# The attention softmax of a fused kernel: normalising multiplies of two blocks on GpSimd, and their weight copy shared by ScalarE and VectorE

## The chip, the cores and the metric

One core of a Trainium2 chip runs the whole program. The metric is device time in microseconds. An engine is named as in the profile: PE is TensorE (PEld its weight loads), DVE is VectorE, ACT is ScalarE, POOL is GpSimd, SP is SyncE, which issues the DMAs here.

## The reference

Windowed causal attention, then two feed-forward layers, all in float32.

```python
scores = q @ k.T / sqrt(64) - slope[h] * (i - j)        # 4 batches, 8 heads, 576 positions
scores = where(0 <= i - j < 128, scores, -1e9)
attn = exp(scores - max); attn = attn / (sum(attn) + 1e-9)
x = concat_heads(attn @ v)                              # 2304 tokens x 512
h = x @ w_in;  x = (h * clip(h + 3, 0, 6) / 6) @ w_out  # 512 -> 2048 -> 512
xn = x / rms(x) * rms_g
out = (silu(xn @ w_gate) * (xn @ w_val)) @ w_out2       # 512 -> 1536 -> 512
```

## The kernel before

The 2304 tokens are 18 tiles of 128 rows, in six blocks of three tiles. Attention works on a pair of heads (`Pair`, four to a block) and one tile of queries (`Step`, three to a pair); both heads of the pair lie side by side in every tile. A step looks at 256 columns of keys (its own tile and the one before), some at 128 or 192 because a batch begins there. One step goes through these pieces, each a method:

- `scores`: q times k on PE, into PSUM.
- `bias` (L367): a DVE instruction for each head adds the slope and the mask and finds the row's extreme `m`.
- `exp` (L382): an ACT instruction for each head gives exp and its row sum `den`. Then POOL makes the reciprocal `r`: an add (L384) and a power of -1 (L385), both on 128x2 values.
- `divide` (L390): each head's tile `t` is multiplied by its column of `r`.
- `transpose` (L396): PE turns `t` into the one PSUM tile `ps_t`.
- `weights` (L401): `ps_t` is copied to SBUF as `pt`.
- `values` (L414): PE multiplies by v.

Every engine takes its instructions in the order in which the code emits them; nothing reorders them. Time is cut into slots by hand. In the first two blocks (pairs 0 to 7, 24 steps) one step begins in each slot, and a step's pieces lie one slot apart: scores, bias and exp in slot t, divide in t+1, transpose and weights in t+2, values in t+3. Slots 0 to 14 are a prologue with attention alone, besides some conversions of weights. From slot 15 on a slot also holds one chunk m of the first feed-forward layer of block 0: `product1` (L480, into `ps_h`), the activation (L717 on ACT, L718 on DVE), its split into a high and a low part (L723 on ACT, L729 on DVE) and `product2` (L493). So the divides of the first two blocks fall into slots 1 to 24, ten of them in the feed-forward loop.

In each of these slots a further tile of weights is converted as well, by ACT (L129, L134, L143) and DVE (L138, L141, L145); `product2` needs the low part that L145 writes. The weights arrive by DMA (L161) from SP, whose queue also loads q, k and v: a load waits there until its buffer is free, and what stands behind it waits too.

Blocks 2 to 5 have a slower plan and masks of another kind (`joint`); they keep their code.

Of the kernel before, what the change touches and what calls it, by code (L numbers as in the profile page):

```python
# [16 lines left out]
ALU = mybir.AluOpType  # L17
# [3 lines left out]
P = 128  # L21
# [50 lines left out]
def fused_kernel(ctx: ExitStack, tc: tile.TileContext, qd, kd, v, w1, w2, rms_g, out):  # L72
# [7 lines left out]
    vec, act, pool, pe, sp = nc.vector, nc.scalar, nc.gpsimd, nc.tensor, nc.sync  # L80
# [245 lines left out]
    class Step:  # L326
# [60 lines left out]
        def divide(self):  # L387
            for a in range(2):
                p = self.t[:, a, self.p0 :]
                vec.tensor_scalar(p, p, self.r[:, a : a + 1], None, ALU.mult)  # L390

        def transpose(self):
            self.ps = ps_a.tile([P, 2, 2, P], F32, tag="T", name="ps_t")
# [4 lines left out]
        def weights(self):  # L398

            self.pt = ap.tile([P, 2, 2, P], F32, tag="pt", name="pt", bufs=3)  # L400
            act.copy(self.pt[:, :, self.p0 // P :], self.ps[:, :, self.p0 // P :])  # L401
            for c, sign in ((0, -1), (1, 1)) if self.joint else ():
                pool.affine_select(  # L403
                    out=self.pt[:, :, c], in_=self.pt[:, :, 1], compare_op=ALU.is_ge, fill=0.0,
                    base=c - 1, pattern=[[0, 2], [sign, P]], channel_multiplier=-sign,
                )
# [592 lines left out]
```

## Time and profile before

| | us |
|---|---|
| median of three runs | 962.07 |
| lowest and highest of them | 959.27, 962.39 |
| the profiled execution | 959.62 |
| its span in the trace | 957.9 |

The profiled execution takes 1.72 us more than its span. A timeline row gives start, duration, engine, line, operation, tiles written and read, count, and in brackets how long the engine had been idle before and what ended that. The chain of waits is followed back from the last instruction: each piece is what the next one waited for.

### The profile page before, as it was taken

The page shows a single profiled execution, that of the slowest core. Times are in us where ns is not written, and L with a number is a line of the kernel's source. Part 1 is how long each engine was busy: PE and PEld are TensorE (multiplying, and loading weights), DVE is VectorE, ACT ScalarE, POOL GpSimd, SP SyncE. Part 2 cuts the span into 40 slices and gives each one's busy share as a digit, 9 for nine tenths or more (in the row PEclk, how much of TensorE's full clock was granted, in tenths as well). Part 3 has the DMA queues.
Part 4 walks back from the last instruction along what each step waited for, and adds up shares of the span by engine and source line. Part 5 has one row for each costly group of instructions (what it writes and reads, how often), then busy time and mean ns, then how long its engine had stood idle before and what let it go on. Part 6 is the DMA issues. An engine that isn't in the chain of part 4 may idle for free.

```text
span 957.9 us, 14648 instructions
## 1 busy us (share of the span) xinstructions
PE 938.1 (98%) x5336; PEld 831.6 (87%) x5336; DVE 642.0 (67%) x1336; ACT 453.6 (47%) x969; POOL 185.2 (19%) x327
## 2 busy tenths in 40 slices
PE   7799899999999999999999999999999999999998
PEld 4587788888888888888898989999999999999996
DVE  5788765555778777877477657777545577545555
ACT  6899764454656655665455453433232323231120
POOL 4333012332223322332034323310000000000000
PEclk8999999999999999999999999999999999999999
DMA  6445601113666554554346757866657655755521
GB/s 225 173 163 192 231 20 33 48 43 108 197 205 218 171 174 144 169 166 154 121 157 232 264 210 281 326 243 233 237 214 283 214 212 200 264 202 209 214 89 67
DMA packets 67432, 175.02 MB, mean 183 GB/s; under 512 B 5024, under 2 KB 41888, under 8 KB 62624
## 3 DMA queue, kind: packets, MB, share of 16 engines
q1 hardware_dynamic: 67360, 174.09, 52.2%
q8 instruction: 42, 0.69, 0.3%
q14 instruction: 30, 0.25, 0.1%
HBM read 130.03 MB, written 44.04 MB: 182 GB/s over the span
## 4 chain that ended last, share of the span: by engine, by line
PE 87%; DVE 5%; ACT 4%; issue 2%; POOL 1%; DMA 1%; SPq 0%; ACTq 0%; POOLq 0%; DVEq 0%
PE ps_o L493 19%; PE ps_h L480 18%; PE ps_y L886 15%; PE ps_o L839 10%; PE ps_S L839 8%; PE ps_A L839 6%; PE ps_h L839 4%; PE ps_av L414 3%; PE ps_t L396 2%; PE ps_s L344 1%; PE ps_s L353 1%; ACT t L382 1%; ACT wx L134 1%; PE ps_x L545 1%; DVE wx L141 1%
## 5 line engine op out<-in xcount | busy, mean ns | idle before, releaser
L493 PE MATMUL ps_o<-w,g 128*128 128x512 f32 x864 | 224.7, 402 | 3.8 <-DVE w L145 2.6
L480 PE MATMUL ps_h<-xs,w 128*128 128x384 f32 x1152 | 220.3, 339 | 0.0
L480 PEld LDWEIGHTS ps_h<-xs,w 128*128 128x128 f32 x1152 | 202.2, 188 | 6.3 <-DVE t L718 0.6
L493 PEld LDWEIGHTS ps_o<-w,g 128*128 128x128 f32 x864 | 156.1, 188 | 43.6 <-DVE w L145 6.0
L886 PE MATMUL ps_y<-wo,g 128*128 128x512 f32 x648 | 150.2, 390 | 0.5 <-DVE g L875 0.5
L886 PEld LDWEIGHTS ps_y<-wo,g 128*128 128x128 f32 x648 | 121.4, 188 | 25.1 <-DVE g L875 0.9
L718 DVE SCALAR_TENSOR_TENSOR t<-t,ps_h 128x384 f32<-128x384 f32 x96 | 53.1, 553 | 99.0 <-ACT t L717 99.0
L717 ACT ACTIVATE t<-ps_h,three 128x384 f32<-128x384 f32 x96 | 55.3, 576 | 79.3 <-PE ps_h L480 76.1
L893 DVE TENSOR_TENSOR y<-y,ps_y 128x512 f32<-128x512 f32 x90 | 61.6, 685 | 35.3 <-PE ps_y L886 35.0
L382 ACT ACTIVATE t<-t,m 128x128 f32<-128x128 f32 (+1 forms) x144 | 61.2, 426 | 29.7 <-DVE t L374 13.5
L723 ACT CAST g<-t 128x384 fp32r<-128x384 f32 x96 | 49.4, 514 | 48.7 <-DVE t L718 47.1
L729 DVE TENSOR_TENSOR g<-t,g 128x384 fp32r<-128x384 f32 x96 | 55.1, 574 | 23.0 <-ACT g L723 22.6
L862 ACT ACTIVATE r<-r 128x384 f32<-128x384 f32 x36 | 18.9, 526 | 105.9 <-DVE r L861 105.9
L839 PE MATMUL ps_o<-S,tw 128*128 128x384 f32 x336 | 66.1, 338 | 0.3 <-DVE t L859 0.3
L384 POOL TENSOR_SCALAR r<-den 128x2 f32<-128x2 f32 x72 | 27.5, 382 | 190.0 <-ACT t L382 188.5
L839 PEld LDWEIGHTS ps_o<-S,tw 128*128 128x128 f32 x336 | 59.3, 188 | 1.2 <-DVE t L859 0.6
L385 POOL TENSOR_TENSOR r<-r,minus 128x2 f32<-128x2 f32 x72 | 55.8, 775 | 6.0
L403 POOL TENSOR_SCALAR_AFFINE_SELECT pt<-pt 128x256 f32<-128x256 f32 x82 | 35.4, 432 | 108.6 <-ACT pt L401 105.6
L847 ACT COPY s<-ps_S 128x384 f32<-128x384 f32 x18 | 8.6, 480 | 88.0 <-PE ps_S L839 88.0
L367 DVE CUSTOM_DVE_ANT_0 t<-ps_s,rel 128x256 f32<-128x256 f32 (+2 forms) x128 | 45.2, 395 | 4.1 <-PE ps_s L353 4.1
L141 DVE SCALAR_TENSOR_TENSOR wx<-wx,wy 128x512 uint32<-128x512 uint32 (+1 forms) x52 | 44.2, 849 | 0.0
L134 ACT ACTIVATE wx<-wraw 128x512 f32<-128x512 f32 (+1 forms) x52 | 42.8, 823 | 0.0
(138 smaller groups left out, 1468.5 us busy)
## 6 DMA issues: line engine op xcount, KB each, us to landing
tw<-t SPq DMA_DIRECT2D x52, 896.0 KB, 6.3
wraw<-w SPq DMA_DIRECT2D x36, 512.0 KB, 4.2
wo<-w SPq DMA_DIRECT2D x18, 1024.0 KB, 4.9
wraw<-w SPq DMA_DIRECT2D x16, 1024.0 KB, 8.4
t<-th SPq DMA_DIRECT2D x12, 896.0 KB, 4.5
t<-tl SPq DMA_DIRECT2D x12, 896.0 KB, 4.2
b<-wx SPq DMA_DIRECT2D x24, 256.0 KB, 2.5
w<-w SPq DMA_DIRECT2D x12, 512.0 KB, 3.0
```

The lines of the kernel that those rows point to most:

```text
L134: act.activation(x, high.bitcast(F32), AF.Copy, scale=2.0**-112)
L141: vec.scalar_tensor_tensor(out=xi, in0=xi, scalar=3, in1=y, op0=ALU.logical_shift_left, op1=ALU.bitwise_or)
L382: act.activation(p, p, AF.Exp, bias=self.m[:, a : a + 1], scale=-1.0, accum_out=self.den[:, a : a + 1])
L385: pool.tensor_tensor(self.r, self.r, minus, ALU.pow)
L480: pe.matmul(ps[:, : n * P], lhsT=w[:, a, c * P : (c + 1) * P], rhs=xs[c][:, b, : n * P], start=(k == 0), stop=(k == 3 * KC - 1),)
L493: pe.matmul(o, lhsT=g[:, a, i * P : (i + 1) * P], rhs=w[:, b], start=(m == first and a == 0 and b == 0), stop=(m == last and a == 1),)
L717: act.activation(r[:, :nq], ps[:, :nq], AF.Relu, bias=three)
L718: vec.scalar_tensor_tensor(out=r[:, :nq], in0=r[:, :nq], scalar=6.0, in1=ps[:, :nq], op0=ALU.min, op1=ALU.mult)
L729: vec.tensor_sub(g[:, 1, :nq], r[:, :nq], f32(g[:, 0, :nq]))
L839: pe.matmul(ps, lhsT=w[a][:, k, c * P : (c + 1) * P], rhs=x[:, b, c], start=(start and j == 0), stop=(j == 5), skip_group_check=True,)
L886: pe.matmul(ps, lhsT=gs[i + k][:, a, t // 3, t % 3 * P : (t % 3 + 1) * P], rhs=wo[i + k][:, b], start=(k == 0 and a == 0 and b == 0), stop ...
L893: vec.tensor_add(acc[t], acc[t], ps)
```

## The change

For blocks 0 and 1 (`pair.b < 2`) the two multiplies of `divide` are issued to POOL and no longer to DVE, and the copy in `weights` is cut by head: ACT copies head 0 and DVE copies head 1. Nothing else moves, and the other blocks are as before. Lines after L401 are numbered up to five higher.

```diff
         def divide(self):
             for a in range(2):
                 p = self.t[:, a, self.p0 :]
-                vec.tensor_scalar(p, p, self.r[:, a : a + 1], None, ALU.mult)
+                (pool if self.pair.b < 2 else vec).tensor_scalar(p, p, self.r[:, a : a + 1], None, ALU.mult)
...
         def weights(self):
...
-            act.copy(self.pt[:, :, self.p0 // P :], self.ps[:, :, self.p0 // P :])
+            c0 = self.p0 // P
+            if self.pair.b < 2:
+                act.copy(self.pt[:, 0, c0:], self.ps[:, 0, c0:])
+                vec.tensor_copy(self.pt[:, 1, c0:], self.ps[:, 1, c0:])
+            else:
+                act.copy(self.pt[:, :, c0:], self.ps[:, :, c0:])
```

On DVE, slots 7 and 8 of the prologue, before (ISA is the bias instruction and its read of `m`):

```order
L367 ISA t,m<-ps_s_369,rel 128x256
L367 ISA m 128x1
L367 ISA t,m<-ps_s_370,rel 128x256
L367 ISA m 128x1
L300 TENSOR_SCALAR qraw<-qraw,qscale 128x384
L390 TENSOR_SCALAR t<-t,r 128x128 x2
L141 SCALAR_TENSOR_TENSOR wx<-wx,wy 128x1024
L367 ISA t,m<-ps_s_398,rel 128x256
```

The same place on DVE now:

```order
L404 COPY pt<-ps_t 128x256
L367 ISA t,m<-ps_s_374,rel 128x256
L367 ISA m 128x1
L367 ISA t,m<-ps_s_375,rel 128x256
L367 ISA m 128x1
L300 TENSOR_SCALAR qraw<-qraw,qscale 128x384
L141 SCALAR_TENSOR_TENSOR wx<-wx,wy 128x1024
L404 COPY pt<-ps_t 128x128
L367 ISA t,m<-ps_s_404,rel 128x256
```

The divide behind the slot's bias is gone, and a copy stands ahead of the slot's bias.

On DVE in a slot of the feed-forward loop (the slot with the rows of 67 us below), before:

```order
L145 TENSOR_TENSOR w<-wx,w 128x1024
L718 SCALAR_TENSOR_TENSOR t<-t,ps_h 128x384
L390 TENSOR_SCALAR t<-t,r 128x256 x2
L367 ISA t,m<-ps_s_901,rel_split 128x256
L367 ISA m 128x1
```

The same place on DVE now (L718 has become L723):

```order
L145 TENSOR_TENSOR w<-wx,w 128x1024
L723 SCALAR_TENSOR_TENSOR t<-t,ps_h 128x384
L404 COPY pt<-ps_t 128x256
L367 ISA t,m<-ps_s_918,rel_split 128x256
L367 ISA m 128x1
```

Between the activation and the bias one copy stands where two multiplies stood.

On POOL at the start of the prologue, before:

```order
L384 TENSOR_SCALAR r<-den 128x2
L385 TENSOR_TENSOR r<-r,minus 128x2
L384 TENSOR_SCALAR r<-den 128x2
L385 TENSOR_TENSOR r<-r,minus 128x2
L384 TENSOR_SCALAR r<-den 128x2
```

On POOL now:

```order
L384 TENSOR_SCALAR r<-den 128x2
L385 TENSOR_TENSOR r<-r,minus 128x2
L390 TENSOR_SCALAR t<-t,r 128x128 x2
L384 TENSOR_SCALAR r<-den 128x2
L385 TENSOR_TENSOR r<-r,minus 128x2
L390 TENSOR_SCALAR t<-t,r 128x256 x2
```

A step's multiplies now follow its own reciprocal directly, ahead of the next step's.

## Rows read from the trace of the kernel before

**Rows 1.** The page: span, and part 1, busy time of each engine.
```profile
span 957.9 us, 14648 instructions
PE 938.1 (98%) x5336; PEld 831.6 (87%) x5336; DVE 642.0 (67%) x1336; ACT 453.6 (47%) x969; POOL 185.2 (19%) x327
```

**Rows 2.** Windows: stretch, length, busy us by engine, clock, DMA share, GB/s.
```profile
20.00:40.00 20.00, 14.05 (x117) 9.03 (x118) 15.54 (x59) 16.73 (x50) 8.63 (x17) 1.00 0.31 92
60.00:80.00 20.00, 19.62 (x118) 15.40 (x115) 17.38 (x37) 18.34 (x34) 6.65 (x7) 1.00 0.60 218
```

**Rows 3.** Chain of waits, one slot of the loop: start, us, what.
```profile
66.52 0.47 ACT t L717
67.02 0.56 DVE t L718
67.57 0.53 DVE t L390 x2
...
72.92 0.47 ACT t L717
```

**Rows 4.** Timeline of PE in one slot of the loop.
```profile
62.65 2.26 PE L480 MATMUL ps_h<-xs,w 128*128 128x384 f32 x12
...
66.49 2.38 PE L493 MATMUL ps_o<-w,g 128*128 128x512 f32 x9
...
68.72 2.28 PE L480 MATMUL ps_h<-xs,w 128*128 128x384 f32 x12
```

**Rows 5.** Timeline, all engines: one turn at the prologue's end.
```profile
35.15 0.52 ACT L382 ACTIVATE t<-t,m 128x256 f32<-128x256 f32 x1
...
36.65 0.70 POOL L385 TENSOR_TENSOR r<-r,minus 128x2 f32<-128x2 f32 x1
...
37.38 0.61 DVE L390 TENSOR_SCALAR t<-t,r 128x256 f32<-128x256 f32 x2 [0.61 <-POOL r L385]
...
37.88 0.63 PE L396 MATMUL ps_t<-ident,t 128*128 128x128 f32 x4 [0.53 <-DVE t L390]
...
38.60 0.58 ACT L401 COPY pt<-ps_t 128x512 f32<-128x512 f32 x1 [0.70 <-PE ps_t L396]
...
39.52 0.46 ACT L382 ACTIVATE t<-t,m 128x192 f32<-128x192 f32 x1
```

**Rows 6.** Line L390 in the whole run: its waits, and who waited for it.
```profile
  POOL r L385: 5.5, 10
...
  PE ps_t L396: 7.0, 7
```

**Rows 7.** Groups by shape, POOL and DVE: count, busy us, mean ns.
```profile
L113 POOL COPY rel_split<-rel 128x256 f32<-128x256 f32 x1 | 0.4, 396 | 0.0
L242 POOL TENSOR_TENSOR tx<-tx 128x256 f32<-128x256 f32 x12 | 9.4, 787 | 0.9
...
L367 DVE CUSTOM_DVE_ANT_0 t<-ps_s,rel 128x256 f32<-128x256 f32 x30 | 11.4, 421 | 2.3 <-PE ps_s L353 2.3
...
L390 DVE TENSOR_SCALAR t<-t,r 128x256 f32<-128x256 f32 x32 | 9.8, 350 | 4.0 <-POOL r L385 4.0
```

**Rows 8.** Timeline of PE, slot 11 of the prologue.
```profile
31.20 0.43 PE L396 MATMUL ps_t<-ident,t 128*128 128x128 f32 x2 [2.37 <-DVE t L390]
```

**Rows 9.** Timeline of POOL and DVE in two slots of the loop.
```profile
64.39 0.96 POOL L385 TENSOR_TENSOR r<-r,minus 128x2 f32<-128x2 f32 x1
...
65.49 1.22 DVE L145 TENSOR_TENSOR w<-wx,w 128x1024 fp32r<-128x1024 f32 x1 [0.17 <-ACT w L143]
...
67.02 0.56 DVE L718 SCALAR_TENSOR_TENSOR t<-t,ps_h 128x384 f32<-128x384 f32 x1 [0.31 <-ACT t L717]
...
75.90 1.22 DVE L141 SCALAR_TENSOR_TENSOR wx<-wx,wy 128x1024 uint32<-128x1024 uint32 x1
...
75.94 1.89 POOL L384 TENSOR_SCALAR r<-den 128x2 f32<-128x2 f32 x1 [3.80 <-ACT t L382]
```

**Rows 10.** Timeline of ACT: the conversion of a tile of weights.
```profile
100.65 1.15 ACT L129 ACTIVATE wy<-wraw 128x1024 uint32<-128x1024 uint32 x1 [1.09 <-DMA wraw<-w]
```

## The prediction

> **What bounds the kernel now.** I read the page first, then the windows, then the chain of waits, then timelines of the two stretches that the change touches. Over the span PE is busy 98% and DVE 67%, ACT 47%, POOL 19% [rows 1]; so for most of the run no other engine matters. The change touches the first 100 us alone, and there the windows say something else: in the prologue (20 to 40 us) PE is busy 14 of 20 us and ACT and DVE 16.7 and 15.5; in the feed-forward loop with attention and conversions (60 to 80 us) PE shows 19.6, ACT 18.3, DVE 17.4, POOL 6.7 [rows 2]. Three engines are nearly full there, and POOL is the idle one. The clock is granted in full in both stretches, so it plays no part.
>
> The chain of waits says which of the three it is. In the loop it runs ACT L717, DVE L718, the two multiplies of L390 (0.53 us), the bias, and so on to the next L717, 6.40 us later [rows 3]. So the multiplies are on the path. But PE is close behind: from product1 to product1 it took 6.07 us in a slot in which it waited for nothing [rows 4]. A loop that gets below 6.07 us becomes PE's. In the prologue the chain goes through one step's pieces in turn: exp on ACT at 35.15, the reciprocal on POOL (done at 36.65 + 0.70 = 37.35), multiplies on DVE from 37.38, transposes from 37.88, the copy on ACT at 38.60, and the exp of the step two slots later at 39.52 [rows 5]. That is a latency chain, and what counts on it is how long each piece takes and what stands ahead of it in its queue, not how full an engine is.
>
> What is saved or lost before about 115 us goes to the end unchanged, since behind it PE runs the same work without a gap. So I add up the two stretches.
>
> **Part 1: the multiplies leave DVE, in the loop.** Ten of the 24 steps have their divide in the loop, so ten slots lose 0.53 us of chain [rows 3] and get the copy of one head in the same place. No row shows a copy out of PSUM on DVE. Nearest is the bias instruction, which reads 128x256 from PSUM in 0.42 us [rows 7]; a pair of multiplies lasts 0.61 us [rows 5] and stands in the chain with 0.53, so neighbours overlap by 0.08 and the copy costs 0.34. It is at least 0.27 (half of 0.53, the price of one multiply), at most 0.42. I take 0.34, since bias reads the same memory. A slot gains 0.53 - 0.34 = 0.19 (0.11 to 0.26), ten slots 1.9.
>
> Not all of it arrives. The slot of 6.07 us was one of three kinds that take turns (a slot without a load's scaling or a block's finish); there PE has no slack, so about three of the ten slots give nothing: 0.6 off. At 100.65 us ACT waited 1.09 us for a tile of weights [rows 10], whose load is released by PE in the slot before last; the time between release and need contains about 1.3 slots, whose 1.3 x 0.19 = 0.25 only lengthens the wait. What is left is 1.9 - 0.6 - 0.25 = 1.05 us gained (0.2 to 2.0).
>
> The multiplies themselves are hidden on POOL here: a reciprocal is ready a whole slot before the transposes that need its product. POOL is busy a third of the time [rows 2], and even 1.6 us for the pair fits. Without that cover each would cost its full time in each slot.
>
> **Part 2: ACT copies half.** In the loop ACT's split of g behind the copy waits for DVE's L718 anyhow, so a shorter copy ends nothing sooner; I cost it at nothing. If L718 were done earlier, it would be worth up to half of the copy's 0.58 us [rows 5] in a slot.
>
> **Part 3: the multiplies on POOL, in the prologue.** No row shows POOL multiplying by a column. One input and one output of 128x256 took POOL 0.40 (the copy), two inputs 0.79 [rows 7]. I take 0.45, the copy and a little for the column and for dispatch, since the multiply too has one large input; ends 0.40 and 0.79. A pair then takes 0.90 where DVE takes 0.61 [rows 5]: 0.29 later. Behind it comes a second loss. The copy on DVE now stands ahead of that slot's bias, and exp comes behind bias; before, exp only stood behind ACT's own copy. Copy 0.34, first bias 0.42 and a hand-over make some 0.85 from transposes to exp, where ACT's copy took 0.55: 0.3 more. So where this chain binds, a turn of two slots loses 0.29 to 0.6.
>
> Where does it bind? PE waited for L390 seven times, 7.0 us in all [rows 6], and only there does a later product come through at once; in other slots conversions on ACT keep the turn longer than the chain. Seven times 0.29 is 2.0, seven times 0.6 is 4.2. Against it stands one place where POOL is better: at 31.20 PE had waited 2.37 us [rows 8] for a divide whose reciprocal was long there, because in DVE's queue a conversion (L145) and a bias stood ahead of it. POOL has neither in its queue. I give back 1.1 of the 2.37, about half, since POOL may have to stand aside while L145 runs; ends 0 and 2.0. DVE's ten waits for the reciprocal, 5.5 us [rows 6], go too, but they return as waits of the copy for the transposes. Prologue: 2.0 - 1.1 = 0.9 us lost (0 to 3).
>
> **The sum.** 0.9 lost and 1.05 gained: -0.15 us. On the profiled execution that is 959.62 - 0.15 = 959.5; on the median, which lies 2.45 us above it, 961.9. The executions shown spread from 959.3 to 962.4, and a new median falls anywhere among them; I say 961.5. About 0.3% (2.9 us) is what a measurement of this kernel can tell from no change, and the sum is far inside it.
>
> **The rivals.**
>
> *A, slower: POOL's multiply is dear.* If the column makes it cost as much as POOL's two-input instruction, 0.79 [rows 7], each of the seven turns loses another 2 x 0.34 = 0.68, together 4.8: 964.3 against the profiled execution, 966.7 against the median. It ends beyond 0.3% from about 0.67 us for a multiply of 128x256 (7 x 2 x 0.22 = 3.1). For it: no row excludes it, and POOL's short power takes 0.70 on two values [rows 5]. Against it: the copy's 0.40. By the Trainium skill (GPSIMD Engine Reference, Key points) elementwise work is about twice as fast on VectorE; as an estimate from that page and the 0.35 of DVE's row the multiply would be 0.70, and the sum 963.0 against the profiled execution.
>
> *B: POOL's multiplies stand in DVE's way.* At 75.94 an add on 128x2 values took POOL 1.89 us, from just after the start of DVE's L141 to the end of the conversion behind it, longer than its neighbour, the power, ever needs when left alone [rows 9]. The two engines thus exclude one another in some instructions. In one kind of slot the power ends at 65.35 and L145 starts at 65.49 [rows 9], so a multiply may slip in first. One puts L145 back by 0.36, two by 0.8; L718 behind had 0.31 to spare [rows 9], so 0.05 or 0.5 is lost, in some four slots up to 2.0. The sum becomes +1.85: 961.5 against the profiled execution, 963.9 against the median. The Trainium skill (SBUF — State Buffer, SBUF: two separate sides) says that VectorE and GpSimd share a pair of ports as an exclusive lock, which whichever begins first holds for the whole instruction; by that rule this loss is real wherever a multiply comes first, and the row of 1.89 us agrees with it.
>
> *C, faster: the engines' fill decides.* If the prologue's turns are set by conversions rather than by latency, POOL's slower multiplies are hidden and only the 1.1 given back counts; if PE's 6.07 us has slack that its modelled ends hide, all 1.9 of the loop arrives. Together -3.0: 956.6 and 959.1. For it: ACT and DVE at 83% and 78% in the prologue [rows 2]. Against it: PE's seven waits.
>
> **How the numbers follow.** The forecast 0.57, of its own range -1.5 to +1.8 us; A 0.15, B 0.12, C 0.16. The range goes from just below C, measured from the median, to between B and A: 958.2 to 965.5; the lowest fifth of C and the dearer half of A are outside. Slower by over 0.3%: nearly all of A and a little of B, 0.16. Faster by over 0.3%: the larger part of C, 0.11. Within: 0.73.
>
> **What would show it.** Part 1: in the loop L718 is followed by a copy of 0.27 to 0.42 us, and three slots take 0.3 to 0.5 us less than before, PE waiting less for L145. Part 3: POOL's multiply of 128x256 at 0.40 to 0.50 us; the first product1 at 39.4 to 40.4 us; bias in the prologue released by the copy, the copy by PE. The wait for weights near 100 us grows by some 0.25 us. A shows as multiplies above 0.65 us and a first product1 beyond 42; B as L145 starting over 0.3 us after ACT's L143; C as a first product1 before 39 us and slots of 6.1 us throughout. The prediction is wrong if the conversions or the loads of weights move onto another path than the one I followed, for instance by a load released so late that ACT waits in every third slot.

## The result and the profile after

The changed kernel takes 970.3 us (median of six, 969.8 to 973.6) against 961.5 for the kernel before in the same rounds: a ratio of 1.0106, 95% interval 1.009 to 1.0123. It is slower by 9 us, and outside the range of 958.2 to 965.5. The profiled execution is the slowest of the six, 973.62 with a span of 971.8; it is 2.6 to 3.8 us longer than the other five, of which there is no trace.

The page: span and part 1, then from part 2 the lines of POOL and of TensorE's granted clock in 40 slices of 24.3 us (compare [rows 1]).

```profile
span 971.8 us, 14658 instructions
...
PE 953.8 (98%) x5336; PEld 839.3 (86%) x5336; DVE 636.8 (66%) x1312; ACT 450.2 (46%) x969; POOL 235.6 (24%) x375
...
POOL 7877411322322322242133133310000000000000
PEclk6589999999999999999999999999999999999999
```

POOL has 50 us more work, more than twice the 22 us that 48 multiplies at the assumed 0.45 would make at most, and in the first slices it is the fullest engine but PE. TensorE's clock is low there. Windows of the changed kernel, columns as in [rows 2], and behind them the first stretch in the kernel before:

```profile
18.00:24.00 6.00, 5.28 (x28) 2.64 (x26) 2.80 (x11) 5.08 (x13) 4.72 (x8) 0.50 0.33 98
...
42.00:48.00 6.00, 5.57 (x26) 2.90 (x26) 2.46 (x11) 2.85 (x10) 5.37 (x9) 0.50 0.06 18
```

```profile
18.00:24.00 6.00, 4.58 (x41) 2.68 (x39) 4.92 (x17) 5.32 (x17) 2.95 (x6) 1.00 0.34 93
```

In these stretches of the prologue POOL is busy 4.7 and 5.4 of 6 us, and the granted clock is 0.50 (of the two levels 1.2 and 2.4 GHz the lower), where before it was 1.00. The timeline of all engines early in the prologue shows what a slot is made of:

```profile
11.04 1.83 POOL L390 TENSOR_SCALAR t<-t,r 128x256 f32<-128x256 f32 x2
...
12.93 0.69 PE L396 MATMUL ps_t<-ident,t 128*128 128x128 f32 x2 [0.21 <-POOL t L390]
12.96 0.22 POOL L384 TENSOR_SCALAR r<-den 128x2 f32<-128x2 f32 x1
13.27 0.72 POOL L385 TENSOR_TENSOR r<-r,minus 128x2 f32<-128x2 f32 x1
...
13.66 0.37 ACT L403 COPY pt<-ps_t 128x256 f32<-128x256 f32 x1 [1.20 <-PE ps_t L396]
14.07 0.42 DVE L404 COPY pt<-ps_t 128x256 f32<-128x256 f32 x1 [2.39 <-ACT pt L403]
14.08 1.83 POOL L390 TENSOR_SCALAR t<-t,r 128x256 f32<-128x256 f32 x2
...
14.41 0.28 DVE L367 CUSTOM_DVE_ANT_0 t<-ps_s,rel 128x128 f32<-128x128 f32 x1
...
14.73 0.40 ACT L382 ACTIVATE t<-t,m 128x128 f32<-128x128 f32 x1 [0.70 <-DVE m L367]
```

Two things are to be seen. The pair of multiplies takes POOL 1.83 us, where DVE took 0.61 [rows 5], and with the add and the power POOL needs 14.08 - 11.04 = 3.04 us for a step: add, power, multiplies, and at once the next add. And the copy on DVE starts not when the transposes are done but when ACT's copy is done (14.07 behind 13.66 + 0.37): its release is ACT's, not PE's. Bias and exp queue behind it.

The waits of DVE over the first 130 us, in total, times, longest, and then those of PE:

```profile
DVE pt L404 <- ACT pt L403: 21.2, 11, 3.1
```

```profile
PE ps_t L396 <- POOL t L390: 6.8, 10, 2.0
```

Eleven times DVE's half of the copy was released by ACT's half. The 21.2 us are all of DVE's idle time ahead of these copies, and most of it passes before the transposes are done: of the 2.39 us in the row above, ACT's copy is the last 0.4. PE now waits for POOL as before for DVE [rows 6]. One slot of the loop on DVE, and then product1 of the loop's first and second slot on PE, in the change and in the kernel before:

```profile
73.41 0.55 DVE L723 SCALAR_TENSOR_TENSOR t<-t,ps_h 128x384 f32<-128x384 f32 x1 [0.32 <-ACT t L722]
73.88 0.42 DVE L404 COPY pt<-ps_t 128x256 f32<-128x256 f32 x1
74.22 0.42 DVE L367 CUSTOM_DVE_ANT_0 t<-ps_s,rel 128x256 f32<-128x256 f32 x1
```

```profile
50.27 4.00 PE L485 MATMUL ps_h<-xs,w 128*128 128x384 f32 x12
55.85 0.44 PE L485 MATMUL ps_h<-xs,w 128*128 128x384 f32 x1
```

```profile
39.03 2.35 PE L480 MATMUL ps_h<-xs,w 128*128 128x384 f32 x12
42.97 2.35 PE L480 MATMUL ps_h<-xs,w 128*128 128x384 f32 x12
```

In the loop the copy costs what I had said: 74.22 - 73.88 = 0.34 us. The first product1 comes at 50.27 us where the kernel before has it at 39.03: that is most of the loss.

Since all later accounts go by it, here is when product1 starts in the first, second and eleventh slot of the loop, for every kernel (us from the span's start), and what lies between the last two. The first column is the length of the prologue, the last the length of nine slots of the loop.

| kernel | first | second | eleventh | nine slots |
|---|---|---|---|---|
| before | 39.03 | 42.97 | 100.18 | 57.21 |
| the change | 50.27 | 55.85 | 112.66 | 56.81 |
| e1, divide only | 49.45 | 54.30 | 109.05 | 54.75 |
| e2, copy only | 46.74 | 50.94 | 111.05 | 60.11 |
| e3, both, loop only | 39.40 | 43.34 | 99.73 | 56.39 |
| e4, the change, PE kept busy | 49.46 | 53.41 | 109.99 | 56.58 |
| e5, divide by a plain number | 44.73 | 48.68 | 103.76 | 55.08 |
| e6, copy only, PE kept busy | 45.87 | 50.09 | 110.18 | 60.09 |
| e7, copy only, two banks | 41.86 | 45.80 | 105.91 | 60.11 |
| e8, copy only, behind bias | 39.60 | 43.57 | 103.67 | 60.10 |
| e9, divide, loop only | 38.94 | 42.89 | 98.01 | 55.12 |
| e10, one head on POOL | 41.97 | 45.91 | 102.06 | 56.15 |

For the profiled execution of the change: 11.24 us in the prologue; 1.64 more in the loop's first slot, whose product1 still ran mostly at the lower clock (4.00 us instead of 2.35; the granted clock was 0.51 over 48 to 54 us); 0.40 gained in nine slots; and 1.5 us lost around 129 us, where the granted clock fell for a moment (0.91 over 120 to 140 us, a product2 of eight matmuls 3.57 us instead of some 2.1). Together that is 14.0, where the span is 13.9 longer. This last fall shows in the profiles of some kernels here and not of others; that it is what sets this execution apart from the other five is not shown.

### The profile page after: what moved, and what is told of

The parts are those of the page before. It is cut to its first block, busy times and chain, and to the rows that moved or that the text cites. A ratio compares the mean times of both kernels' runs of the same rounds, so it can differ in the third digit from the quotient of the medians.

```text
span 971.8 us, 14658 instructions
## 1 busy us (share of the span) xinstructions
PE 953.8 (98%) x5336; PEld 839.3 (86%) x5336; DVE 636.8 (66%) x1312; ACT 450.2 (46%) x969; POOL 235.6 (24%) x375
## 4 chain that ended last, share of the span: by engine, by line
PE 84%; DVE 6%; ACT 5%; issue 2%; POOL 2%; DMA 1%; SPq 0%; ACTq 0%; POOLq 0%; DVEq 0%
PE ps_o L498 18%; PE ps_h L485 17%; PE ps_y L891 15%; PE ps_o L844 10%; PE ps_S L844 8%; PE ps_A L844 6%; PE ps_h L844 4%; PE ps_av L419 2%; PE ps_t L396 2%; PE ps_s L353 1%; ACT wx L134 1%; ACT t L382 1%; PE ps_s L344 1%; POOL t L390 1%; DVE wx L141 1%
## 5 line engine op out<-in xcount | busy, mean ns | idle before, releaser
L485 PEld LDWEIGHTS ps_h<-xs,w 128*128 128x128 f32 x1152 | 204.3, 190 | 6.1 <-issue 0.3
L723 DVE SCALAR_TENSOR_TENSOR t<-t,ps_h 128x384 f32<-128x384 f32 x96 | 53.1, 553 | 101.8 <-ACT t L722 101.7
L390 POOL TENSOR_SCALAR t<-t,r 128x256 f32<-128x256 f32 (+2 forms) x48 | 48.9, 1029 | 2.3
L396 PE MATMUL ps_t<-ident,t 128*128 128x128 f32 x190 | 40.2, 311 | 7.1 <-POOL t L390 6.8
```

What stands on the lines that cost most here:

```text
L390: (pool if self.pair.b < 2 else vec).tensor_scalar(p, p, self.r[:, a : a + 1], None, ALU.mult)
L396: pe.transpose(self.ps[:, a, c], self.t[:, a, c * P : (c + 1) * P], ident)
L485: pe.matmul(ps[:, : n * P], lhsT=w[:, a, c * P : (c + 1) * P], rhs=xs[c][:, b, : n * P], start=(k == 0), stop=(k == 3 * KC - 1),)
L723: vec.scalar_tensor_tensor(out=r[:, :nq], in0=r[:, :nq], scalar=6.0, in1=ps[:, :nq], op0=ALU.min, op1=ALU.mult)
```

## The experiments

**e1 to e4: which edit, which stretch, and the clock.**

e1 undoes the copy's split, e2 the move of the multiplies:

```diff
# e1
-            if self.pair.b < 2:
+            if False:
                 act.copy(self.pt[:, 0, c0:], self.ps[:, 0, c0:])
# e2
-                (pool if self.pair.b < 2 else vec).tensor_scalar(p, p, self.r[:, a : a + 1], None, ALU.mult)
+                vec.tensor_scalar(p, p, self.r[:, a : a + 1], None, ALU.mult)
```

Expected of e1:

> The multiplies on GpSimd, the copy whole on ScalarE as before. Theory P (GpSimd's multiply, 0.92 us instead of 0.35, fills GpSimd's queue in the prologue): most of the loss of 9 us stays, 967 to 971 us, first product1 at 46 to 50 us. Theory S (VectorE's half of the copy, which waits for ScalarE's half and holds up bias): the loss goes, 960 to 964 us.

Measured: 970.7 us, ratio 1.0107 (1.009 to 1.0124). Theory P: the multiplies alone bring the whole loss. POOL in e1, from the prologue's first multiplies:

```profile
8.59 1.21 POOL L390 TENSOR_SCALAR t<-t,r 128x128 f32<-128x128 f32 x2
...
11.01 1.84 POOL L390 TENSOR_SCALAR t<-t,r 128x256 f32<-128x256 f32 x2
12.93 0.22 POOL L384 TENSOR_SCALAR r<-den 128x2 f32<-128x2 f32 x1
13.24 0.72 POOL L385 TENSOR_TENSOR r<-r,minus 128x2 f32<-128x2 f32 x1
14.05 1.84 POOL L390 TENSOR_SCALAR t<-t,r 128x256 f32<-128x256 f32 x2
...
45.88 1.84 POOL L390 TENSOR_SCALAR t<-t,r 128x256 f32<-128x256 f32 x2
```

POOL hardly rests: from 8.6 to 51 us it waited for ACT twice, 0.77 us in all. So the prologue is POOL's queue. From 8.59, where the multiplies of step 0 begin, to 45.88, where those of step 12 do, lie twelve steps: four of 128 columns at 2.4 us (1.2 for the pair) and eight of 256 at 3.04 make 33.9 us; 2.9 are POOL's instructions taking longer than usual while DVE's L138, L141, L145 and L300 run, 0.5 a wait for ACT: together the 37.3. Transposes and values follow, and the loop's first product1 at 49.45.

Expected of e2:

> The multiplies on VectorE as before, the copy split. Theory P: near the kernel before, 960 to 964 us, first product1 at 39 to 41 us. Theory S: 965 us or more, first product1 past 42 us.

Measured: 972.1 us, ratio 1.0121 (1.0106 to 1.0136). So theory P fails here and theory S holds: the copy's split alone costs as much as the whole change. Each edit is enough for the loss, and together they don't add up: in the change POOL waited for ACT 2.9 us up to 52 us, where in e1 it was 0.8, so its queue is nearly as full as in e1, and most of the copy's loss passes while POOL is busy. e2's timeline, all engines, one copy and what follows:

```profile
24.04 0.37 ACT L403 COPY pt<-ps_t 128x256 f32<-128x256 f32 x1 [0.83 <-PE ps_t L396]
24.45 0.42 DVE L404 COPY pt<-ps_t 128x256 f32<-128x256 f32 x1 [1.46 <-ACT pt L403]
24.79 0.41 DVE L367 CUSTOM_DVE_ANT_0 t<-ps_s,rel 128x256 f32<-128x256 f32 x1
...
25.31 0.51 ACT L382 ACTIVATE t<-t,m 128x256 f32<-128x256 f32 x1 [0.89 <-DVE m L367]
```

From the start of the copy to exp are 1.27 us; before, ACT's copy took that place alone, some 0.55 [rows 5]. e2's prologue is 7.7 us longer, its loop 2.9 (copies and multiplies both on DVE).

e3 makes both edits for the loop's steps alone (`14 <= self.k < 24` for the multiplies, `13 <= self.k < 24` for the copies, with `self.k` the number of the step):

> Both edits only for the ten divides and eleven copies that fall into the feed-forward loop; the prologue as before. If the loss is all the prologue's (theory P, and the prediction's sum for the loop): 959 to 961.5 us, first product1 at 39.0 us as before, a gain of 0 to 1 us. If GpSimd's multiplies also cost something in the loop by standing in VectorE's way (rival B): 962 to 966 us.

Measured: 960.9 us, ratio 1.0005 (0.9996 to 1.0014). The nine slots are 0.82 us shorter, and by the thirteenth product1 it is 1.0 ahead from the first one on (110.88 - 39.40 against 111.52 - 39.03). So the loss is the prologue's, and the loop does gain what it should. The gain then went in this profile: the granted clock fell at 118 us, and product1 took

```profile
118.16 2.93 PE L486 MATMUL ps_h<-xs,w 128*128 128x384 f32 x12
```

instead of 2.27. Over ten runs nothing is left that can be measured.

e4 keeps TensorE busy in the prologue:

```diff
         scores(s_, t % 2)
+        busy(2)
```

> The changed kernel with two more matmuls of 128x256 in each prologue slot, into a PSUM bank that is idle there, so that TensorE stays busy. Theory C (the loss comes from TensorE at half its clock for 12 to 54 us): granted clock 1.0 from some 20 us on, first product1 below 44 us, 961 to 965 us. Theory P (GpSimd's queue sets the slots whatever the clock): first product1 at 47 to 50 us, 967 to 970 us.

Measured: 971.8 us, ratio 1.0112 (1.0096 to 1.0128). Windows of e4:

```profile
18.00:24.00 6.00, 5.00 (x36) 3.25 (x34) 3.04 (x13) 5.15 (x13) 5.10 (x8) 1.00 0.42 142
24.00:30.00 6.00, 5.68 (x43) 3.77 (x40) 3.80 (x16) 3.11 (x12) 5.25 (x8) 1.00 0.24 67
```

The clock is whole from the start and the first product1 comes at 49.46, 0.81 us earlier than in the change; with the loop's first slot it is 2.4. PE still waited for POOL ten times, 4.9 us in all. The time lies 1.8 us above theory P's range, but the loss is all there at the full clock: theory C falls. The lower clock went away when PE had more to do, so it came of PE's idle time and is not what sets the prologue.

**e5 to e8: why each edit costs what it does.**

e5 is e1 with a plain number; it leaves out the normalisation of the attention weights:

```diff
-                (pool if self.pair.b < 2 else vec).tensor_scalar(p, p, self.r[:, a : a + 1], None, ALU.mult)
+                (
+                    pool.tensor_scalar(p, p, 1.0, None, ALU.mult)
+                    if self.pair.b < 2
+                    else vec.tensor_scalar(p, p, self.r[:, a : a + 1], None, ALU.mult)
+                )
```

> As the divide-only kernel, but GpSimd multiplies by the number 1.0 instead of a column of reciprocals, so the attention weights are not normalised; same shapes, same queue places. Theory P1 (the column operand makes GpSimd's multiply dear, and this price sets the prologue): a multiply of 128x256 takes 0.40 to 0.50 us, first product1 at 39 to 42 us, 960 to 963 us. Theory P2 (any multiply of this shape costs GpSimd some 0.9 us): 0.9 us, first product1 at 48 to 50 us, 969 to 971 us.

Measured: 965.9 us, ratio 1.0051 (1.0034 to 1.0068). Neither is right. POOL in e5:

```profile
8.45 1.05 POOL L391 TENSOR_SCALAR t<-t 128x128 f32<-128x128 f32 x2
...
10.58 1.68 POOL L391 TENSOR_SCALAR t<-t 128x256 f32<-128x256 f32 x2
12.33 0.22 POOL L384 TENSOR_SCALAR r<-den 128x2 f32<-128x2 f32 x1
12.64 0.72 POOL L385 TENSOR_TENSOR r<-r,minus 128x2 f32<-128x2 f32 x1
13.33 0.86 POOL L391 TENSOR_SCALAR t<-t 128x256 f32<-128x256 f32 x1
...
42.04 1.68 POOL L391 TENSOR_SCALAR t<-t 128x256 f32<-128x256 f32 x2
```

A multiply by a number still takes 0.84 (1.68 for two), so it is the instruction that is dear, and the column adds only 0.08. But a step costs POOL 13.33 - 10.58 = 2.75 instead of 3.04 us, for the multiplies also follow the power without the gap of 0.09, and the prologue is 4.7 us shorter. From the multiplies of step 0 to those of step 12 e5 needs 42.04 - 8.45 = 33.6 us, 3.7 less than e1, and twelve steps times 0.29 are 3.5: the prologue follows POOL's time per step almost one to one. That is the queue, measured a second way. Of the other 1.0 us, 0.9 lies between the multiplies of step 12 and product1 (2.69 instead of 3.57), where the granted clock was 0.96 in e5 and 0.50 in e1.

e6 is e2 with `busy(2)` as in e4:

> The copy-only kernel with two more matmuls of 128x256 per prologue slot, to keep TensorE's clock up. Theory C2 (the copy-only loss of 8 us in the prologue is half the clock's): product1 at 41 to 43 us, 4 us or more back. Theory S (VectorE's copy waiting for ScalarE's, ahead of bias): product1 at 45 us or later, 969 us or more.

Measured: 971.3 us, ratio 1.0105 (1.0088 to 1.0121); first product1 at 45.87, 0.87 us earlier, clock 1.0. Theory S.

e7 is e2 with the second head's transposes of the prologue in a PSUM bank of their own (the bank of `ps_out` o2, idle there):

```diff
+            if self.k < 13:
+                self.heads = [ps_a.tile([P, 2, P], F32, tag="T", name="ps_t"), ps_out.tile([P, 2, P], F32, tag="o2", name="ps_t2")]
...
-                vec.tensor_copy(self.pt[:, 1, c0:], self.ps[:, 1, c0:])
+                vec.tensor_copy(self.pt[:, 1, c0:], self.heads[1][:, c0:])
```

> The copy-only kernel with the second head's transposes of the prologue in a PSUM bank of their own, so that VectorE's copy waits for TensorE alone and not for ScalarE's copy of the same bank. Theory S1 (the wait of 0.4 us for ScalarE's half makes the loss): product1 at 41 to 43 us. Theory S2 (it is the copy's place ahead of bias in VectorE's queue): product1 at 44 to 46 us, at most 2 us back.

Measured: 965.3 us, ratio 1.0044 (1.0029 to 1.0059); first product1 at 41.86, so 4.9 of 7.7 us come back. That is S1's range; S2's 44 to 46 fails. Waits of DVE in the first 60 us in e2, then in e7, then in e8:

```profile
DVE pt L404 <- ACT pt L403: 12.0, 11, 1.5
```

```profile
DVE pt L412 <- PE ps_t L404: 6.8, 10, 1.5
```

```profile
DVE pt L417 <- ACT pt L404: 4.5, 9, 1.0
```

In e7 the copy waits for PE alone, and 5.2 us less than in e2, about what comes back. `pt` is one tile in both kernels, so the wait for ACT was one for the shared `ps_t`, whose two halves are different columns of one PSUM bank. No run has two tiles in one bank, so tile and bank are not told apart here. The Trainium skill (PSUM — Partial Sum Buffer, PSUM bank collisions raise a hardware error) states that two engines may not touch the same bank in the same partitions at once, not even both reading, and that their accesses must be ordered; the trace of the change agrees, with DVE's half released by ACT's in eleven copies, and so does e7, where such waits are gone.

e8 is e2 with DVE's half of the prologue's copies issued behind the slot's bias:

```diff
         for x in s_:
             x.bias()
+        for x in t_:
+            x.second()
```

> The copy-only kernel with VectorE's half of the prologue's copies issued behind the slot's bias instead of ahead of it; banks as in the change. Theory S2: product1 at 39 to 41 us, 5 us or more back. Theory S1: product1 still past 44 us, as the copy waits for ScalarE's half wherever it stands.

Measured: 963.4 us, ratio 1.0031 (1.0021 to 1.0041); first product1 at 39.60, 7.1 of 7.7 us back, though the wait for ACT's half is still there. That is S2's range; S1's condition (still past 44) fails. So each theory failed in one of the two runs: the copy is dear by its place ahead of bias, and 4.9 of the 7.7 us are the wait for ACT's half, which counts only in that place. What remains in e8 is the loop, 2.9 us for copies on top of multiplies.

**e9 and e10: what POOL can take.**

e9 leaves all copies to ACT and moves only the loop's ten pairs of multiplies:

```diff
-                (pool if self.pair.b < 2 else vec).tensor_scalar(p, p, self.r[:, a : a + 1], None, ALU.mult)
+                (pool if 14 <= self.k < 24 else vec).tensor_scalar(p, p, self.r[:, a : a + 1], None, ALU.mult)
```

> GpSimd multiplies for the ten steps whose divide falls into the feed-forward loop; prologue and all copies as before. Theory P with TensorE as the loop's next bound (slots of 6.08 us, as the divide-only kernel's loop has them, against 6.36 before): first product1 at 39.0 us, the eleventh about 2.4 us earlier than before, 958 to 959.5 us, faster than the kernel before. Rival B (GpSimd in VectorE's way): no gain or a loss, 960.5 us or more.

Measured: 958.7 us against 960.1, ratio 0.9988 (0.9979 to 0.9997): a little faster than the kernel before. PE in e9:

```profile
42.89 2.38 PE L486 MATMUL ps_h<-xs,w 128*128 128x384 f32 x12
...
98.01 2.29 PE L486 MATMUL ps_h<-xs,w 128*128 128x384 f32 x12
```

Nine slots of 6.12 us instead of 6.36: close to PE's 6.07 [rows 4]; PE waits there 0.3 us in all, before 1.6. Of the 2.1 us, 1.1 remain in the span, 956.8 against 957.9: behind the eleventh product1 PE waits 1.7 us for L145 where it waited 1.0, and 0.5 for ACT's copy where it waited 0.2.

e10 puts one head's multiplies on POOL and leaves the other on DVE (`self.pair.b < 2 and a`), copies on ACT:

> Of the two heads one is multiplied on VectorE and one on GpSimd, in all 24 steps; copies as before. Theory P as a queue (GpSimd's time per step sets the slots once it exceeds them): GpSimd needs some 2.1 us per step instead of 3.0, less than a slot of 2.26, so the first product1 comes at 39.5 to 42 us and most of the loss is gone: 959.5 to 962.5 us. If instead the latency of one multiply on the chain counted (theory L): half of the loss stays, product1 at 44 to 46 us, 964 to 967 us.

Measured: 964.1 us, ratio 1.005 (1.0034 to 1.0067). The first product1, 41.97, lies at the edge of what the queue theory gave, the time 1.6 us above it. POOL in e10:

```profile
10.39 1.08 POOL L390 TENSOR_SCALAR t<-t,r 128x256 f32<-128x256 f32 x1
11.55 0.23 POOL L384 TENSOR_SCALAR r<-den 128x2 f32<-128x2 f32 x1
11.86 0.72 POOL L385 TENSOR_TENSOR r<-r,minus 128x2 f32<-128x2 f32 x1
12.68 1.08 POOL L390 TENSOR_SCALAR t<-t,r 128x256 f32<-128x256 f32 x1
```

A single multiply takes 1.08, so a step is 2.29 us, not the 2.1 that I had worked out from half a pair, and that is just the average slot of before, (39.03 - 5.09) / 15 = 2.26, in which POOL then has no room for delays. Half of the multiplies cost 2.9 us of prologue, all of them 10.4: not half, as by latency, but what lies above a limit.

## Why the prediction was wrong

**Where the kernel is bound** was read rightly in the main: the loss and the gain arise before 115 us, PE is the loop's next bound, and the prologue is a chain through the engines. But "goes to the end unchanged" is too strong: of e9's 2.1 us about half goes into PE's waits behind the loop.

**Part 1, the loop**, held in its terms. The copy costs 0.34 us on the chain, as taken. The loop-only kernel e3 gained 0.8 to 1.0 us against the 1.05 worked out, the change itself 0.40 in nine slots, inside the range of 0.2 to 2.0; the multiplies alone give 2.1 to 2.5 over nine slots (e9, e1), and the copy on DVE costs 2.9 where it comes on top (e2).

**Part 3 is the step that failed, in two terms.** "I take 0.45": the multiply of 128x256 takes POOL 0.92 in a pair and 1.08 alone, above both ends that I had, 0.40 and 0.79. The copy was the wrong neighbour, and so was the idea that the column would be what a multiply has extra: it adds 0.08 of 0.92 (e5). DVE's 0.35 [rows 7] went to 0.92, a factor of 2.6. The factor of two of the Trainium skill (GPSIMD Engine Reference, Key points) was nearer than mine and still short of the measurement.

With the true price my own formula would give 7 x 2 x 0.47 = 6.6 us more, and it would still have been the wrong formula. I asked where POOL's latency binds and found seven places. At 3.04 us a step POOL is slower than the slot of 2.26, and then it binds in every slot: **"what counts on it is how long each piece takes ..., not how full an engine is"** was the sentence that misled me. POOL at 8.63 us busy in 20 [rows 2] looked idle; for each step of 2.26 us it already had some 1.0 of add and power (1.03 in e1's rows; [rows 5] show the power, 0.70), and a pair at 0.92 each makes nearly three. At the price of 0.45 it would have fitted, so the sum hung on that one unseen number more than its ends told. The 1.1 us given back, because POOL's queue has no L145 in it, did not arrive either: that queue was full, and an instruction of POOL took 0.8 us longer while L141 or L145 ran (e1).

**The copy** was the second term of Part 3: "0.3 more" a turn for its place ahead of bias. The place was seen, but not that DVE's half must wait for ACT's half of the same bank, so that the 0.3 became 0.7 (1.27 us from copy to exp in e2, where I had 0.85 and before 0.55). Nor did the sum count this loss: it took seven times 0.29, for the multiplies alone, and left the 0.3 to the upper end of the range without a reason. Alone the copy costs 7.7 us of prologue (e2).

**The rivals.** A was the right mechanism in kind, POOL's multiply is dear, with the condition "above 0.65 us and a first product1 beyond 42" fulfilled; but it too counted seven turns, and its prices, 0.79 and 0.70, lie below the 0.92, so its 964.3 to 966.7 us fall short of the 970.3. B did not happen. In the change a multiply began just ahead of L145 and L145 was not put back:

```profile
59.25 2.88 POOL L390 TENSOR_SCALAR t<-t,r 128x256 f32<-128x256 f32 x2
59.28 1.23 DVE L145 TENSOR_TENSOR w<-wx,w 128x1024 fp32r<-128x1024 f32 x1 [0.17 <-ACT w L143]
```

L145 takes its usual 1.23 us [rows 9] and POOL's pair 2.88 instead of 1.83: it is POOL that stands aside, which in the loop costs nothing. The rule of the Trainium skill (SBUF — State Buffer, SBUF: two separate sides), that whichever begins first holds the ports, would have it the other way round, if the recorded start is where POOL takes them; the measurement decides. C's direction was wrong for this change: the prologue's turns were set by POOL and not by conversions. Its slots of 6.1 us do come in e9, where the multiplies leave DVE and no copy takes their place; the shortest of them is 5.94, so PE's 6.07 holds little slack.

What stays open is the fall of the granted clock near 118 to 130 us in some profiles (before, e5, e6, e8, e9 and e10 are without it): it costs 1.5 us in the change and 0.9 in e3, and none of these runs says what brings it.

## What to carry to other kernels

Before work goes to an idle engine, divide its queue by the pace of the stage: add what it already does per step to the new work at the dearest price that can't be excluded, and see whether it stays below the step's length; beyond that it sets every step, not just those where it was waited for. Where only a stretch has the slack (here the loop, not the prologue), move only that stretch's work, as e9 does. And an instruction that is put on a second engine brings its waits into that engine's queue: look at what stands behind it, and whether both halves read one PSUM bank.

## What was unexpected of the hardware

- POOL's multiply: 0.60 us for 128 columns, 0.92 for 256 in pairs, some 2.5 ns a column, whereas its copy of 256 took 0.40 [rows 7]. A column of scalars adds only 0.08.
- Where POOL's work met DVE's conversions, only POOL's got longer: 2.88 us for the pair instead of 1.83, while L145 kept its 1.23.
- TensorE's granted clock was 0.50 through most of the change's prologue, in which PE often waited for POOL, and 1.00 with two added matmuls a slot (e4); the full clock brought only 0.8 us of prologue.
